# First pair's weight sums on GpSimd, one quarter sum later, and two kinds of request earlier, in an attention and FFN kernel

## Chip, core and metric

One core of a Trainium2 chip runs the whole kernel. The metric is the device time of one execution in microseconds (us); lower is better. Five engines work side by side: TensorE (PE, with its weight loads as PEld), VectorE (DVE), ScalarE (ACT), GpSimd (POOL) and SyncE (SP), which here only issues transfers. Each runs its own instructions strictly in the order in which they were queued, and an instruction that waits for a semaphore holds back everything behind it on that engine.

## What is computed

A linear attention over 8 x 8 heads of 576 tokens, and then a feed-forward layer over all 4608 tokens:

```python
def phi(x):
    proj = np.einsum('bhsd,df->bhsf', x, w_phi)
    proj = proj - np.max(np.abs(proj), axis=-1, keepdims=True)
    return np.concatenate([np.exp(proj), np.exp(-proj)], axis=-1)
q_p, k_p = phi(q), phi(k)
kv = np.einsum('bhsf,bhsd->bhfd', k_p, v)
num = np.einsum('bhsf,bhfd->bhsd', q_p, kv)
den = np.einsum('bhsf,bhf->bhs', q_p, np.sum(k_p, axis=2))[..., None] + 1e-06
x = (num / den).transpose(0, 2, 1, 3).reshape(4608, 512)
h = x @ w_in                                    # 512 -> 2048
g = np.maximum(h, 0.0) + alpha * np.minimum(h, 0.0)
out = g @ w_out                                 # 2048 -> 512
```

## The kernel before

Up to about 340 us the attention runs, 32 pairs of heads one after the other; its output goes to `x_d` in DRAM, and the two weights, decoded on the way, to `u_d` and `v_d`. What matters here is what follows, the feed-forward layer. Its tokens are nine chunks of 512 columns. Every fp32 operand is split into a rounded high part (a cast on ACT, `rnd`, L139) and a low part (the original less the high one, on DVE, `low`, L143), and a product is three matmuls, high by high, low by high, high by low (L546 to L548, L556 to L558, and L833 to L835).

**Chunk 0 is done plainly**, from 340 to 422 us. Hidden blocks of 128 rows alternate between an up step of 12 matmuls (`up2`, L546 to L548), the activation (`act_g`: r on ACT at L258, g on DVE at L262, high part gh on ACT, low part gl on DVE), and a down step of 12 matmuls (`down2`, L556 to L558) on gh and gl.

**Chunks 1 to 8 are done as four pairs** with a Strassen-Winograd scheme: seven products in place of eight. A pair has an up phase of eight units (`unit`). The seven products of a unit run in the order A12, S2, S1, S3, then the first product A11 of the next unit, then S4 and A22; pa, pb and pc are their PSUM tiles, and between the products ACT copies (COPY pb<-pa at L889, u and p at L845) and applies r (L853), while DVE adds (L849) and makes g (L854). A down phase (`down_pair`) follows, seven products over eight operands hv each; an operand is a cast on ACT and a low on DVE, now and then with a subtract on DVE.

**The scheme needs sums of weight quarters** besides the plain ones. `sums` makes one set: load the four quarters with a DMA from `a_d` on POOL's queue (L675); four 128x256 adds and subtracts on DVE (`two` and `four`, L682, L683, L688, L689); two halves, each a cast on ACT and a low on DVE (`half0`, `half1`); and two stores on POOL's queue (L703) to `us_d` and `vs_d`. Up-weight sums are su, down-weight sums sv. There are 16 sets: the first nine, in `work[:9]`, are made during chunk 0 at places that a table of offsets, `SUMT`, gives; the last seven (sv of units 6 and 7, su of units 3 to 7) are made during the first pair's up phase. For those su sets unit 3 to 7 of the first pair reads S1 to S4 straight from the halves that the set leaves in SBUF. `"hv" in late` is true for exactly these seven.

**x for the next pair** is loaded during a down phase: `prepare` gives, for each of j = 0 and 1, a load of the first half (xr, L760), and seven pieces, each an optional subtract (L778), a cast to xo and a low; the first piece also asks for the second half. One entry is taken from that list after each operand that `PIECES` names. From the second pair on, the loads of j = 0 and j = 1 share one buffer, so xr_1 is asked for only when DVE has read the last of xr_0.

**What sets the order:** PE, SP and POOL run as the program is written. ACT and DVE are reordered by the framework's scheduler, which holds, with `behind`, the sums and pieces behind the newest instruction of that engine. So a change in one place can move rows of ACT and DVE nearby.

Of the kernel before, what the change touches and what calls it, by code (L numbers as in the profile page):

```python
# [12 lines left out]
ALU = mybir.AluOpType  # L13
# [13 lines left out]
NU = NF // 2  # L27
# [8 lines left out]
NLAST = 4  # L36
NNEXT = 5
UX = 2
PIECES = [(k, u) for k in range(1, 7) for u in range(NU)][4 : 4 + 48 : 3]
NPRE = 2  # L40
W_BUFS = 2
RW_BUFS = 4
# [62 lines left out]
HEAD = 4  # L105
# [5 lines left out]
UPA = 2  # L111
SUM0, SUMD = 1.5, 3.0
SUMT = dict(load=-5.0, two=0.0, four=0.2, half0=0.6, half1=0.8, store0=1.5, store1=1.6)
SUMS = [(0, 0), (0, 1), (1, 0), (1, 1), (2, 0), (2, 1), (3, 1), (4, 1), (5, 1), (6, 1), (7, 1)]
NSUM = 9
NJIT = 3
# [5 lines left out]
def fused_kernel(ctx: ExitStack, tc: tile.TileContext, kq, v, w_phi, w_in, w_out, alpha, out):  # L122
    nc = tc.nc
    act, dve, pool, pe = nc.scalar, nc.vector, nc.gpsimd, nc.tensor
# [9 lines left out]
    def f(t):  # L134
        return t.bitcast(F32)

    def rnd(eng, dst, src):
        if eng is act:
            return act.copy(dst, src)  # L139
        return eng.tensor_copy(dst, src)  # L140

    def low(eng, dst, src, hi):
        return eng.tensor_tensor(dst, src, f(hi), op=ALU.subtract)  # L143
# [13 lines left out]
    late = {}  # L157
# [92 lines left out]
    def behind(eng):  # L250
        return tc.issue_after(newest[eng].ins) if eng in newest and "pso" in late else ExitStack()
# [343 lines left out]
    todo = []  # L595
# [19 lines left out]
    def load_up(p, u):  # L615
        if p:
            parts = (("wa", 2, A11, 2), ("ws", 2, S1, 3), ("ws", 2, S3, 3), ("wb", 1, A22, 2))
        else:
            parts = (("wa", 2, A11, 2), ("ws", 2, A21, 3))
        for tag, k, n, bufs in parts:  # L620
            if p == 1 and u >= NJIT and tag == "ws":
                continue
            t = late["wu"].tile([P, k, 2, WN], F32R, tag=tag, name=f"{tag}{p}_{u}_{n}", bufs=bufs)
            src = us_d[u, :, UPL[n] : UPL[n] + k] if n >= S3 else u_d[u, :, n : n + k]
            nc.sync.dma_start(f(t), src)
            for j in range(k):
                wu[p, u, {S1: (S1, S2), S3: (S3, S4)}.get(n, (n, n + 1))[j]] = t[:, j]
# [31 lines left out]
    def sums(u, down):  # L659
        k = "v" if down else "u"  # L660
        st = {}

        def new(n):
            name = f"s{k}_{u}_{n}"
            if "hv" in late:
                if n and not down:
                    return late["wu"].tile([P, 4 * WN], F32, tag="ws", name=name, bufs=3)
                return late["hv"].tile([P, 4 * WN], F32, tag="hv", name=name, bufs=NH)
            if n:
                return w1t.tile([P, 4 * WN], F32, tag="wraw", name=name, bufs=RW_BUFS)  # L670
            return late["s"].tile([P, 4 * WN], F32, tag="s", name=name, bufs=3)

        def load():
            a = new(0).rearrange("p (n c) -> p n c", n=4)
            pool.dma_start(a, a_d[int(down), u])  # L675
            st["b"] = [a[:, n] for n in ((0, 2, 1, 3) if down else (A11, A12, A21, A22))]
            st["src"] = (a[:, 0:2], a[:, 2:4]) if down else (a[:, 1:3], a[:, 0:4:3])

        def two():
            a11, a12, a21, a22 = st["b"]  # L680
            with behind("dve"):
                dve.tensor_tensor(a22, a21, a22, op=ALU.add)  # L682
                dve.tensor_tensor(a21, a11, a21, op=ALU.subtract)  # L683

        def four():
            a11, a12, a21, a22 = st["b"]
            with behind("dve"):
                dve.tensor_tensor(a11, a22, a11, op=ALU.subtract)  # L688
                dve.tensor_tensor(a12, a12, a11, op=ALU.subtract)  # L689

        def half(n):
            a = st["src"][n]
            t = st[n] = new(n + 1).bitcast(F32R).rearrange("p (n t c) -> p n t c", t=2, c=WN)
            with behind("act"):
                rnd(act, t[:, :, 0], a)
            with behind("dve"):
                low(dve, t[:, :, 1], a, t[:, :, 0])
            if "hv" in late and not down:
                for j, s in enumerate(((S1, S2), (S3, S4))[n]):
                    wu[1, u, s] = t[:, j]  # L700

        def store(n):
            pool.dma_start((us_d, vs_d)[down][u, :, 2 * n : 2 * n + 2], f(st[n]))  # L703

        parts = dict(load=load, two=two, four=four)
        parts |= {f"half{n}": lambda n=n: half(n) for n in range(2)}
        return parts | {f"store{n}": lambda n=n: store(n) for n in range(2)}
# [6 lines left out]
    def glu2(c, ff, n):  # L714
        r = gq[c, ff][n]()
        if n == 3:
            gq[c, ff] = r
# [34 lines left out]
    def prepare(p):  # L752
        c = 2 * p - 1
        todo = []
        for j in range(2):
            b = {}
            cut = p == 1 and not j

            def half(k, b=b):
                (pool if p == 1 else nc.sync).dma_start(b["raw"][:, k], b["src"][:, k])  # L760

            def load(j=j, b=b, cut=cut, half=half):
                raw = late["x2" if j and p == 1 else "xt"].tile([P, 2, 2 * C2], F32, tag="xr", name=f"xr{p}_{j}", bufs=1)
                src = x_d.rearrange("(k j) p s -> j p k s", j=2)[j][:, :, c * C2 : (c + 2) * C2]
                b["raw"], b["src"] = raw, src
                if not cut:
                    half(0)
                for k in range(2):
                    for t in range(2):
                        b[k, t] = raw[:, k, t * C2 : (t + 1) * C2]  # L770

            def quarter(k, t, j=j, b=b):
                nc.sync.dma_start(b[k, t], x_d[2 * k + j, :, (c + t) * C2 : (c + t + 1) * C2])

            def piece(n, src, x=None, j=j, b=b):
                if x is not None:
                    with behind("dve"):
                        dve.tensor_tensor(b[src], b[x[0]], b[x[1]], op=ALU.subtract)  # L778
                t = late["xo"].tile([P, 2, C2], F32R, tag=f"x{n}_{j}", name=f"xo{p}_{n}_{j}")
                with behind("act"):  # L780
                    rnd(act, t[:, 0], b[src])
                with behind("dve"):
                    low(dve, t[:, 1], b[src], t[:, 0])
                xo[p, n, j] = (t[:, 0], t[:, 1])

            steps = [(A11, (0, 0)), (S1, (0, 0), ((0, 1), (0, 0))), (A12, (1, 0)), (S4, (1, 1))]
            steps += [(S3, (0, 1), ((1, 1), (0, 1))), (S2, (1, 1), ((1, 1), (0, 0))), (A22, (1, 0), ((1, 0), (1, 1)))]
            todo.append(load)
            if cut:
                todo += [lambda k=k, t=t, quarter=quarter: quarter(k, t) for k in range(2) for t in range(2)]  # L790
            more = [] if cut else [half]
            for st_ in steps:
                todo.append(lambda st_=st_, piece=piece, more=more: ([h(1) for h in more[:1]], more.clear(), piece(*st_)))
        return todo

    order = [("u", k) for k in range(HEAD)]
# [5 lines left out]
    for n, (k, ff) in enumerate(order):  # L802
        t = HEADS[n] if n < HEAD else t1 + (n - HEAD) * U2
        if k == "d":
            todo.append((t, lambda ff=ff: down2(ff)))
            if ff + 2 * NPRE < NF:
                todo.append((max(t + 0.0005, (WDT + (0,) * NF)[ff]), lambda ff=ff + 2 * NPRE: load_down(ff)))
            continue
        todo.append((t, lambda ff=ff: up2(0, ff)))
        if n >= HEAD and ff % 2 and ff // 2 + UPA < NU:  # L810
            todo.append((t + 0.0006, lambda u=ff // 2 + UPA: load_up(0, u)))
        for i, dt in enumerate(GH.get(ff, (0, *GQ))):
            todo.append((t + U2 - 0.01 + dt, lambda ff=ff, i=i: glu2(0, ff, i)))
    for u in range(NOWN, HEAD // 2 + UPA):
        todo.append((t1 + 0.0001 + 2.5 * U2 * (u > NOWN), lambda u=u: load_up(0, u)))
    work = [sums(*x) for x in SUMS] + [sums(u, 0) for u in range(NJIT, NU)]
    for n, parts in enumerate(work[:NSUM]):
        for k, dt in SUMT.items():
            todo.append((max(t1 + 0.0002, t1 + (SUM0 + SUMD * n + dt) * U2 + 0.002), parts[k]))
    for n, t in enumerate(XPT + tuple(t1 + (XP0 + XPD * n) * U2 + 0.003 for n in range(11))):  # L820
        todo.append((t, lambda n=n: (prep.extend(prepare(1) if n == 0 else []), pieces(1))))
    todo.append((t1 + 5 * U2, lambda: prep.pop(4)()))
    end = t1 + (len(order) - HEAD) * U2 - 0.002
    todo.append((end, lambda: load_up(1, 0)))
    todo.append((end + 10, turn_on))
    todo.sort(key=lambda tu: tu[0])
    for late_part, engines in ((False, pinned), (True, {et.PE, et.SP, et.Pool})):
# [90 lines left out]
    hv, wv = {}, {}  # L918
# [36 lines left out]
    def down_pair(p):  # L955
# [4 lines left out]
        for k, n in enumerate(ORDER):  # L960
# [8 lines left out]
            for u, m in um:  # L969
# [11 lines left out]
                if m == turn and k + u:  # L981
                    some_operand()
                    if (k, u) in PIECES:
                        pieces(1)
# [117 lines left out]
```

## Time and profile before

| | us |
|---|---|
| median of 3 runs | 1013.92 (1013.58 to 1015.92) |
| the profiled execution | 1014.1 |
| its span | 1012.3 |
| PE busy in the span | 994.4 |
| DVE busy | 787.8 |
| ACT busy | 606.6 |
| POOL busy | 242.0 |

The span runs from the first instruction to the last; 1.8 us lie around it. Busy time counts the time in which an engine executes something; an engine's idle time before an instruction is put down to what that instruction waited for last. The granted clock is TensorE's, as a share of full speed.

### The profile page before, as it was taken

How to read it: one execution, taken by the hardware profiler on the slowest of the kernel's cores; microseconds unless marked ns; L12 is line 12 of the kernel's file. 1: busy time of each engine (PE TensorE's matmuls, PEld its weight loads, DVE VectorE, ACT ScalarE, POOL GpSimd, SP SyncE). 2: the span in 40 equal slices, each digit the busy share in tenths (PEclk: the TensorE clock that was granted, in tenths of full speed). 3: DMA queues.
4: the chain of work that ended last, by engine and by line, in shares of the span. 5: the costliest groups of instructions: out<-in, count | busy, mean ns of one | idle time of the engine just before them, and what ended most of it. 6: DMA issues, size and time to landing. Idle time of an engine off the chain costs nothing.

```text
span 1012.3 us, 18434 instructions
## 1 busy us (share of the span) xinstructions
PE 994.4 (98%) x6881; PEld 804.6 (79%) x6881; DVE 787.8 (78%) x1238; ACT 606.6 (60%) x1163; POOL 242.0 (24%) x218
## 2 busy tenths in 40 slices
PE   9999999999999989999999999999999999999998
PEld 7666666766676878887888888888888888888887
DVE  7999999999997767689997565897465887465874
ACT  4787878787786534455565444566454565444553
POOL 0565656666575322122000000000000000000001
PEclk9999999999999999999999999999999999999999
DMA  5677888898886599988768665768566768565565
GB/s 178 214 282 273 290 282 294 278 331 293 293 288 215 186 352 408 398 307 336 284 223 272 201 217 194 264 223 273 183 229 222 253 207 307 175 210 196 180 220 182
DMA packets 99336, 258.47 MB, mean 255 GB/s; under 512 B 12656, under 2 KB 13296, under 8 KB 99248
## 3 DMA queue, kind: packets, MB, share of 16 engines
q1 hardware_dynamic: 88816, 221.71, 64.1%
q0 software_dynamic: 10000, 35.39, 9.1%
q8 instruction: 54, 0.88, 0.4%
q14 instruction: 34, 0.28, 0.1%
q10 hardware_dynamic: 432, 0.20, 0.1%
HBM read 196.16 MB, written 60.96 MB: 254 GB/s over the span
## 4 chain that ended last, share of the span: by engine, by line
PE 83%; DVE 4%; DMA 3%; ACT 0%; issue 0%; SPq 0%; ACTq 0%; DVEq 0%
PE kv L387 5%; PE n L452 5%; PE qa L835 5%; PE qa L834 5%; PE qa L833 5%; PE pa L833 5%; PE pa L834 5%; PE pa L835 5%; PE pj L347 4%; PE pc L835 3%; PE pc L834 3%; PE pc L833 3%; PE qc L835 2%; PE d L470 2%; PE qc L833 2%; PE qc L834 2%
## 5 line engine op out<-in xcount | busy, mean ns | idle before, releaser
L139 ACT CAST hv<-g 128x512 fp32r<-128x512 f32 x224 | 135.8, 619 | 88.4 <-PE qa L835 43.7
L143 DVE TENSOR_TENSOR hv<-g,hv 128x512 fp32r<-128x512 f32 x224 | 150.8, 687 | 42.0 <-ACT hv L139 41.1
L725 POOL DMA_DIRECT2D out_dram<-pt x35 | 19.0, 543 | 504.6 <-ACT pt L1001 416.7
L835 PE MATMUL qa<-hv,wv 128*128 128x512 f32 (+1 forms) x257 | 97.3, 379 | 0.0
L834 PE MATMUL qa<-hv,wv 128*128 128x512 f32 (+1 forms) x257 | 97.2, 378 | 0.0
L833 PE MATMUL qa<-hv,wv 128*128 128x512 f32 (+1 forms) x257 | 97.2, 378 | 0.0
L351 DVE TENSOR_REDUCE m<-pj 128x8 f32<-128x1024 f32 (+2 forms) x67 | 78.3, 1169 | 5.3 <-PE pj L347 5.3
L352 DVE TENSOR_TENSOR t<-pj,m 128x1024 f32<-128x1024 f32 (+2 forms) x67 | 78.9, 1177 | 4.4
L347 PEld LDWEIGHTS pj<-w_sb,raw 64*128 64x128 f32 x1024 | 63.2, 190 | 17.5 <-issue 13.9
L200 POOL TENSOR_TENSOR aw<-ew,aw 128x512 f32<-128x512 f32 x32 | 41.1, 1285 | 143.3 <-DVE ew L196 143.3
L347 PE MATMUL pj<-w_sb,raw 64*128 64x128 f32 x1024 | 72.7, 282 | 2.3 <-DVE t L352 1.8
L374 POOL TENSOR_TENSOR y<-xk 128x1024 f32<-128x1024 f32 x30 | 70.9, 2364 | 0.0
L452 PE MATMUL n<-qf,sf 128*64 128x288 f32 x512 | 69.2, 412 | 0.0
L366 ACT ACTIVATE xk<-t 128x1024 f32<-128x1024 f32 (+1 forms) x66 | 65.8, 1072 | 4.9 <-DVE t L352 4.9
L443 ACT ACTIVATE qf<-qt 128x512 f32<-128x512 f32 x128 | 66.7, 633 | 0.0
L853 ACT ACTIVATE r<-g 128x512 f32<-128x512 f32 x65 | 37.4, 622 | 47.4 <-DVE g L849 47.4
L387 PE MATMUL kv<-xk,v 128*64 128x256 f32 x512 | 62.3, 385 | 0.0
L463 ACT COPY s<-n 128x288 f32<-128x288 f32 x64 | 25.3, 399 | 58.3 <-PE n L452 58.3
L854 DVE SCALAR_TENSOR_TENSOR g<-r,al,g 128x512 f32<-128x512 f32 x65 | 46.3, 748 | 17.8 <-ACT r L853 17.8
L139 ACT CAST xo<-xr 128x512 fp32r<-128x512 f32 x56 | 34.1, 621 | 40.0 <-DVE xr L778 19.7
L835 PEld LDWEIGHTS qa<-hv,wv 128*128 128x128 f32 x257 | 48.6, 189 | 7.1 <-DVE hv L143 0.2
L833 PEld LDWEIGHTS qa<-hv,wv 128*128 128x128 f32 x257 | 48.6, 189 | 6.9
(195 smaller groups left out, 2586.3 us busy)
## 6 DMA issues: line engine op xcount, KB each, us to landing
wv<-vs_d SPq DMA_DIRECT2D x64, 512.0 KB, 4.4
ws<-us_d SPq DMA_DIRECT2D x54, 512.0 KB, 4.7
wv<-v_d SPq DMA_DIRECT2D x48, 512.0 KB, 4.3
wa<-u_d SPq DMA_DIRECT2D x37, 512.0 KB, 6.2
raw<-kq_dram SPq DMA_DIRECT2D x31, 576.0 KB, 5.0
v<-v_dram SPq DMA_DIRECT2D x32, 320.0 KB, 4.2
rr<-rec_d SPq DMA_DIRECT2D x64, 144.0 KB, 3.2
x_d<-rr SPq DMA_DIRECT2D x32, 288.0 KB, 2.5
```

Of the source, the lines that this page charges most:

```text
L139: return act.copy(dst, src)
L143: return eng.tensor_tensor(dst, src, f(hi), op=ALU.subtract)
L347: pe.matmul(dst[h, j], lhsT=c["raw"][hs, ts], rhs=w_sb[hs], start=True, stop=True)
L351: dve.tensor_reduce(m, src, axis=AX.X, op=ALU.max, apply_absolute_value=True)
L352: dve.tensor_tensor(t[:, hs, js], src, m.unsqueeze(3).broadcast_to([P, nh, nj, FD]), op=ALU.subtract)
L374: pool.tensor_tensor(y, x[:, :, : 2 * FD], x[:, :, 2 * FD :], op=ALU.add)
L387: pe.matmul(c["kv"][h * D : (h + 1) * D, 0:2], lhsT=c["v"][:, tp, h, :], rhs=c["x", ch][:, :, h, j, :], start=tp == 0, stop=tp == NV - 1,)
L443: act.activation(c["qf"][:, h, a, : 4 * P], ps.rearrange("p j f -> p (j f)"), AF.Exp, scale=sg)
L452: pe.matmul(ps[h * D : (h + 1) * D, :], lhsT=c["st"][:, a, h * D : (h + 1) * D], rhs=c["qf"][:, h, a, u * HS : (u + 1) * HS], start=a == 0 ...
L833: pe.matmul(ps, lhsT=wh, rhs=xh, start=first, stop=False, skip_group_check=True)
L834: pe.matmul(ps, lhsT=wl, rhs=xh, start=False, stop=False, skip_group_check=True)
L835: pe.matmul(ps, lhsT=wh, rhs=xl, start=False, stop=end, skip_group_check=True)
```

## The change

Four edits:

1. The four adds of a set go to POOL for the seven sets of the first pair (`adder`). The other nine stay on DVE.
2. For the set n = 1 of the table (sv of unit 0), the second half and its store come at 2.2 and 2.6 slots instead of 0.8 and 1.6 (`SUML`).
3. The first pair's first weights, `load_up(1, 0)`, are asked for at an entry of chunk 0's table, behind the up step of block 13, instead of at the table's end.
4. In the down phases the entries of the x list are taken at `PIECES[1::3]` instead of `[4:52:3]`, three operands sooner; for pairs 2 to 4 an empty entry in front of j = 1's pieces keeps the last ones where they were.

```diff
-PIECES = [(k, u) for k in range(1, 7) for u in range(NU)][4 : 4 + 48 : 3]
+PIECES = [(k, u) for k in range(1, 7) for u in range(NU)][1::3]
...
+SUML = dict(half1=2.2, store1=2.6)
...
+        def adder():
+            return (pool, ExitStack()) if "hv" in late else (dve, behind("dve"))
+
         def two():
             a11, a12, a21, a22 = st["b"]
-            with behind("dve"):
-                dve.tensor_tensor(a22, a21, a22, op=ALU.add)
-                dve.tensor_tensor(a21, a11, a21, op=ALU.subtract)
+            eng, order = adder()
+            with order:
+                eng.tensor_tensor(a22, a21, a22, op=ALU.add)
+                eng.tensor_tensor(a21, a11, a21, op=ALU.subtract)
...
             todo.append(load)
+            if p > 1 and j:
+                todo.append(lambda: None)
...
-        if n >= HEAD and ff % 2 and ff // 2 + UPA < NU:
-            todo.append((t + 0.0006, lambda u=ff // 2 + UPA: load_up(0, u)))
+        if n >= HEAD and ff % 2 and ff // 2 + UPA <= NU:
+            u = ff // 2 + UPA
+            todo.append((t + 0.0006, lambda x=(0, u) if u < NU else (1, 0): load_up(*x)))
...
-        for k, dt in SUMT.items():
+        for k, dt in (SUMT | SUML if n == 1 else SUMT).items():
             todo.append((max(t1 + 0.0002, t1 + (SUM0 + SUMD * n + dt) * U2 + 0.002), parts[k]))
...
-    todo.append((end, lambda: load_up(1, 0)))
```

`four` is changed in the same way as `two`. The lines of the changed kernel are numbered a few higher.

The queues around unit 3 of the first pair, POOL first. Here sv_0_5584 is the set of down weights of unit 7, su_0_5586 the set of up weights of unit 3; _1 and _2 are their two halves. Before:

```order
L675 DMA su_0_5668<-a_d 128x1024 [waits DMASW4_49,DMASW2_49]
L703 DMA vs_d<-sv_1_5674 128x1024 [waits DMASW3_49,DVE_49]
L703 DMA vs_d<-sv_2_5719 128x1024 [waits DVE_49]
L675 DMA su_0_5755<-a_d 128x1024 [waits DMASW5_49,DMASW1_49]
L703 DMA us_d<-su_1_5761 128x1024 [waits DMASW6_49]
```

and after:

```order
L695 TENSOR_TENSOR sv_0_5584<-sv_0_5584 128x256 [waits Pool_49]
L709 DMA vs_d<-sv_1_5674 128x1024 [waits DMASW3_49,DVE_49]
L709 DMA vs_d<-sv_2_5719 128x1024 [waits DVE_49]
L676 DMA su_0_5755<-a_d 128x1024 [waits Pool_49]
L687 TENSOR_TENSOR su_0_5586<-su_0_5586 128x256 [waits DMASW6_49]
L688 TENSOR_TENSOR su_0_5586<-su_0_5586 128x256 [waits Pool_49]
L694 TENSOR_TENSOR su_0_5586<-su_0_5586 128x256 [waits Pool_49]
L695 TENSOR_TENSOR su_0_5586<-su_0_5586 128x256 [waits Pool_49]
L709 DMA us_d<-su_1_5761 128x1024 [waits DVE_49]
```

The four adds of the set su_0_5586 now stand on POOL behind two stores that wait for DVE and behind a load.

ACT in the same place (pb_3 is unit 3's copy of pa; r_1_2 and r_1_3 are activations of units 2 and 3). Before:

```order
L889 COPY pb_2_5731<-pa_2_5724 128x512 [waits PE_49]
L139 CAST su_1_5761<-su_0_5586 128x2x256 [waits DMAHW3_49,DMAHW0_49,DMAHW4_49,DMASW6_49,DMAHW7_49,DVE_49,PE_49]
L853 ACTIVATE r_1_1_5740<-g_1_5691 128x512 [waits DVE_49,Activation_49]
...
L139 CAST su_2_5803<-su_0_5586 128x2x256 [waits DMAHW7_49,DMAHW2_49,DMAHW0_49]
L139 CAST sv_1_5674<-sv_0_5584 128x2x256 [waits DMASW5_49,DMASW0_49]
L139 CAST sv_2_5719<-sv_0_5584 128x2x256 [waits DVE_49]
L889 COPY pb_3_5815<-pa_3_5808 128x512 [waits PE_49]
```

and after:

```order
L140 CAST sv_1_5674<-sv_0_5584 128x2x256 [waits DMASW5_49,DMASW0_49,Pool_49]
L897 COPY pb_3_5815<-pa_3_5808 128x512 [waits DVE_49,PE_49]
L140 CAST sv_2_5719<-sv_0_5584 128x2x256 [waits DMASW1_49,Pool_49]
...
L861 ACTIVATE r_1_3_5860<-pb_3_5815 128x512 [waits DVE_49,PE_49]
L140 CAST su_1_5761<-su_0_5586 128x2x256 [waits DMAHW3_49,DMAHW4_49,DMAHW0_49,DMAHW7_49,DMASW6_49,Pool_49]
L140 CAST su_2_5803<-su_0_5586 128x2x256 [waits DMAHW2_49,DMAHW7_49,DMAHW0_49,Pool_49]
L853 COPY u_1_3_5869<-pa_3_5808 128x512 [waits PE_49]
```

The cast of unit 3's S1 and S2 moved from behind COPY pb_2 to behind COPY pb_3 and two more sets of rows, and the cast sv_2_5719 moved behind COPY pb_3. Further down, in the same way, the casts su_1_5845 and su_2_5887 come to stand ahead of COPY pb_4 of the next unit, and su_2_5887 waits there for the landing of the store of su_1_5761 (its buffer).

ACT during chunk 0, at hidden block 4 (r_0_4 and gh_0_4 belong to its activation, sv_2 is the second half of set n = 1). Before:

```order
L139 CAST sv_1_4989<-sv_0_4865 128x2x256 [waits DMASW1_49,DMAHW5_49,DVE_49,Activation_49]
L139 CAST sv_2_4994<-sv_0_4865 128x2x256 [waits DMAHW5_49,DVE_49,Activation_49]
L258 ACTIVATE r_0_4_4967<-h_0_4_4950 128x512 [waits PE_49]
L139 CAST gh_0_4_5000<-g_0_4_4992 128x512 [waits DVE_49]
L139 CAST xo_7_0_5024<-xr_0_2889 128x512
```

and after:

```order
L140 CAST sv_1_4989<-sv_0_4865 128x2x256 [waits DMASW1_49,DMAHW5_49,DVE_49,Activation_49]
L259 ACTIVATE r_0_4_4967<-h_0_4_4950 128x512 [waits PE_49]
L140 CAST gh_0_4_4997<-g_0_4_4992 128x512 [waits DVE_49]
L140 CAST xo_7_0_5020<-xr_0_2889 128x512
L140 CAST sv_2_5023<-sv_0_4865 128x2x256 [waits DMAHW5_49,Activation_49]
```

The second half's cast stands behind the activation of block 4 instead of ahead of it; its low on DVE moved in the same way behind g, gl and xo_7.

In the down phase, on SP, before (xr_1 is the load of x with j = 1):

```order
L927 DMA wv_4_2_6638<-vs_d 128x2x512 [waits DMAHW0_49,PE_49]
L927 DMA wv_4_3_6668<-vs_d 128x2x512 [waits DMAHW1_49,PE_49]
L760 DMA xr_1_6688<-x_d 128x1024 [waits DVE_49]
L927 DMA wv_5_0_6690<-vs_d 128x2x512 [waits DMAHW2_49,PE_49]
L927 DMA wv_5_1_6710<-vs_d 128x2x512 [waits DMAHW3_49,PE_49]
```

and after:

```order
L935 DMA wv_4_2_6642<-vs_d 128x2x512 [waits DMAHW0_49,PE_49]
L766 DMA xr_1_6653<-x_d 128x1024 [waits DVE_49]
L935 DMA wv_4_3_6670<-vs_d 128x2x512 [waits DMAHW1_49,PE_49]
L935 DMA wv_5_0_6690<-vs_d 128x2x512 [waits DMAHW2_49,PE_49]
L935 DMA wv_5_1_6710<-vs_d 128x2x512 [waits DMAHW3_49,PE_49]
```

xr_1's first half is asked for one weight load sooner. On ACT its first cast, xo_2_1, moved from behind the casts of hv_4_6 and hv_4_7 to ahead of them. SP's rows for `load_up(1, 0)` stand where they stood.

## Rows read from the trace of the kernel before

**Rows 1.** The page: busy time, share of the span and instructions of each engine.

```profile
PE 994.4 (98%) x6881; PEld 804.6 (79%) x6881; DVE 787.8 (78%) x1238; ACT 606.6 (60%) x1163; POOL 242.0 (24%) x218
```

**Rows 2.** Waits of PE, 330 to 1000 us: total, times, longest.

```profile
PE po L556 <- ACT gh L139: 3.2, 1, 3.2
PE qc L835 <- DVE hv L143: 2.9, 3, 1.3
PE pa L833 <- DVE g L854: 1.7, 1, 1.7
PE pa L833 <- DMA wa<-u_d: 1.4, 1, 1.4
```

**Rows 3.** Timeline of chunk 0, block 4: start, duration, instruction, idle before and releaser.

```profile
357.61 0.62 ACT L139 CAST sv<-sv 128x512 fp32r<-128x512 f32 x1 [3.80 <-DMA v_d<-raww]
...
358.26 0.69 DVE L143 TENSOR_TENSOR sv<-sv,sv 128x512 fp32r<-128x512 f32 x1 [3.72 <-ACT sv L139]
...
360.31 0.48 PE L556 MATMUL po<-gh,wd 128*128 128x512 f32 x1 [3.16 <-ACT gh L139]
```

**Rows 4.** Stretches: length, busy time of each engine (instructions), granted clock, DMA share, GB/s.

```profile
core 0: us, PE busy (x) PEld busy (x) DVE busy (x) ACT busy (x) POOL busy (x), PEclk, DMA share, GB/s
350.00:375.00 25.00, 21.81 (x93) 18.17 (x92) 15.48 (x26) 8.73 (x15) 8.81 (x13) 0.93 0.97 345
...
400.00:426.00 26.00, 26.00 (x121) 22.47 (x120) 20.42 (x37) 14.57 (x27) 5.85 (x11) 1.00 1.02 411
...
361.40:364.80 3.40, 3.40 (x10) 2.68 (x9) 2.72 (x6) 0.83 (x2) 0.00 (x0) 0.50 1.04 389
...
451.00:493.00 42.00, 40.27 (x187) 34.79 (x186) 37.92 (x67) 25.29 (x47) 7.64 (x15) 1.00 0.91 325
```

**Rows 5.** Timeline: the first pair's first weights reach PE.

```profile
414.35 0.19 PEld L833 LDWEIGHTS pa<-xo,wa 128*128 128x128 f32 x1 [0.39 <-DMA wa<-u_d]
```

**Rows 6.** Timeline of the first pair, units 3, 4 and 6: copies and products.

```profile
447.73 0.57 ACT L889 COPY pb<-pa 128x512 f32<-128x512 f32 x1
...
451.41 0.38 PE L833 MATMUL pa<-xo,su 128*128 128x512 f32 x1
...
456.79 0.57 ACT L889 COPY pb<-pa 128x512 f32<-128x512 f32 x1 [2.00 <-PE pa L835]
...
475.41 0.48 PE L833 MATMUL pa<-xo,wa 128*128 128x512 f32 x1 [1.73 <-DVE g L854]
```

**Rows 7.** POOL's groups by line, and one DVE group of 428 to 493 us: count, busy, mean ns.

```profile
L374 POOL TENSOR_TENSOR y<-xk 128x1024 f32<-128x1024 f32 x30 | 70.9, 2364 | 0.0
L200 POOL TENSOR_TENSOR aw<-ew,aw 128x512 f32<-128x512 f32 x32 | 41.1, 1285 | 143.3 <-DVE ew L196 143.3
L703 POOL DMA_DIRECT2D us_d<-su x16 | 8.5, 535 | 30.3 <-DVE su L143 30.1 <-issue 0.2
...
L854 DVE SCALAR_TENSOR_TENSOR g<-r,al,g 128x512 f32<-128x512 f32 x14 | 10.2, 747 | 0.8 <-ACT r L853 0.8
...
L683 DVE TENSOR_TENSOR su<-su 128x256 f32<-128x256 f32 x5 | 2.1, 422 | 0.1
```

**Rows 8.** Timeline: an add on POOL and an add on DVE at the same time.

```profile
351.27 1.56 POOL L501 TENSOR_TENSOR rr<-s,rr 128x576 f32<-128x576 f32 x1 [7.98 <-DMA rr<-rec_d]
...
351.60 1.52 DVE L688 TENSOR_TENSOR sv<-sv 128x256 f32<-128x256 f32 x1
```

**Rows 9.** Stores of su, 440 to 480 us: time from issue to landing.

```profile
DMA to landing us min/median/max: 2.9/6.7/11.4
```

**Rows 10.** Timeline of the first pair's down phase: load, cast, low, PE.

```profile
538.28 0.46 SPq L760 DMA_DIRECT2D xr<-x_d  x1
...
546.55 0.62 ACT L139 CAST xo<-xr 128x512 fp32r<-128x512 f32 x1 [4.17 <-DMA xr<-x_d]
...
547.20 0.69 DVE L143 TENSOR_TENSOR xo<-xr,xo 128x512 fp32r<-128x512 f32 x1 [4.10 <-ACT xo L139]
...
555.34 0.48 PE L835 MATMUL qc<-hv,wv 128*128 128x512 f32 x1 [1.34 <-DVE hv L143]
```

More of the change, by code (lines that the diff above doesn't have):

```diff
@@ L677, in load @@
             st["src"] = (a[:, 0:2], a[:, 2:4]) if down else (a[:, 1:3], a[:, 0:4:3])
+        def adder():
+            return (pool, ExitStack()) if "hv" in late else (dve, behind("dve"))
         def two():
             a11, a12, a21, a22 = st["b"]
-            with behind("dve"):
-                dve.tensor_tensor(a22, a21, a22, op=ALU.add)
-                dve.tensor_tensor(a21, a11, a21, op=ALU.subtract)
+            eng, order = adder()
+            with order:
+                eng.tensor_tensor(a22, a21, a22, op=ALU.add)
+                eng.tensor_tensor(a21, a11, a21, op=ALU.subtract)
         def four():
             a11, a12, a21, a22 = st["b"]
-            with behind("dve"):
-                dve.tensor_tensor(a11, a22, a11, op=ALU.subtract)
-                dve.tensor_tensor(a12, a12, a11, op=ALU.subtract)
+            eng, order = adder()
+            with order:
+                eng.tensor_tensor(a11, a22, a11, op=ALU.subtract)
+                eng.tensor_tensor(a12, a12, a11, op=ALU.subtract)
         def half(n):
```

## Prediction, made before the changed kernel had run

> **What bounds the kernel now.** First the page: PE is busy 994.4 of 1012.3 us [rows 1]. What an edit gives or costs is therefore read from the gaps of PE, not from the busy time of the engine that it relieves. Second, who PE waits for after 330 us [rows 2]: 3.2 us once for ACT's cast gh, 2.9 us in three pieces for DVE's low of hv, 1.7 us once for DVE's g, 1.4 us once for a load of weights, 9.2 us in all. Third, the timeline around each gap, to see which instruction stood in front of the one that PE waited for [rows 3, 5, 6, 10]. Fourth, stretches with the clock and the DMA share [rows 4]: only once after 330 us is the clock low, 0.50 in 361.40 to 364.80, right behind the 3.16 us gap; 3.4 us at 1.2 instead of 2.4 GHz lose about 1.7 us, and behind the gap of 1.73 us no such stretch lies.
>
> **Edit 2, the quarter sum in chunk 0.** It removes a block. ACT stood 3.80 us in front of the cast of sv because that cast waits for the landing of a store; r of block 4 stood behind it on ACT and g behind the low of sv on DVE, which sat idle 3.72 us, then gh, and PE waited 3.16 us for that [rows 3]. With the cast behind gh, r and g need not wait for the landing, and the half clock has no gap to follow. PE would then lead the old times by some 3.2 + 1.7 = 4.9 us. The lead is spent on the way. The DMA share is 0.97 from 350 to 375 us and 1.02 from 400 to 426, with 345 and 411 GB/s [rows 4], and the first weights of the first pair came just when PE wanted them: PE's weight load waited 0.39 us for wa and began at 414.35 [rows 5]. A DMA system without a pause can't deliver sooner, and edit 3 doesn't help, as SP's rows stand in the same order. The only reserve is the 0.03 x 25 = 0.75 us by which the share of 350 to 375 stays below one. I take -0.5 us. Ends: -4.9 if other transfers can give way to the weights, and +2 if the lead is lost in one gap over 3 us, with another stretch of low clock.
>
> **Edit 1, POOL adds in the first pair.** It removes 28 adds of 0.42 us, 11.8 us, from DVE [rows 7], and with them the 1.73 us at 475.41, where PE waited for DVE's g [rows 2, 6]: DVE is busy 37.92 of 42 us from 451 to 493 [rows 4]. So -1.7 us.
>
> What it adds is 28 adds on POOL. The trace has none of 128x256; 128x1024 takes 2.36 and 128x512 1.29 us [rows 7], on a straight line 0.75 us for 128x256, 3.0 us for the four of a set. POOL has room; its order is the trouble. I follow unit 3's S2, which reads the half su_1 of the set su_0_5586. Before, DVE did it early and PE began S2 at 451.41 without a wait [rows 6]. After, its four adds stand on POOL behind the stores of sv_1_5674 and sv_2_5719, and the second of these waits for a cast that ACT does behind COPY pb_3. The copy starts at 447.73 and takes 0.57 [rows 6], to 448.3; the cast 0.62 and low 0.69 [rows 3], to 449.6; the store and the next load, 0.54 each, as the stores of us_d [rows 7], to 450.7; four adds, 3.0, to 453.7; the cast of su_1, 0.62, to 454.3. PE wants it at 451.41: a wait of 2.9, and 0.4 more before the second matmul, which needs the low part: 3.3 us. While the adds run, DVE makes two g of 0.75 from SBUF [rows 7]; that one engine holds the other up is seen at 351.60, where an add of DVE took 1.52 instead of 0.42 while POOL ran 1.56 [rows 8]. If the two g hold up POOL in the same way, it is 3.3 + 1.5 = 4.8. I take 4.0. A gap of this size is nearer to the 3.16 us gap than to the 1.73 one, so I add a stretch of low clock, 1.7 us, with 0 as the other end.
>
> The next term is unit 4. The cast of su_2_5887 now stands ahead of COPY pb_4 and waits for the landing of the store of su_1_5761. Stores here take 2.9 to 11.4 us, 6.7 in the middle [rows 9]. The store goes out at about 455.5, so it lands between 458.4 and 466.9, at 462.2 in the middle; the copy of unit 4 came at 456.8, one unit of seven products or 9.1 us after that of unit 3 [rows 6], and with the delays above (4.0 + 1.7) is wanted at 462.5. PE waits nothing at the middle and 4.4 at the upper end; I take 1.5. Units 5 to 7 have the same shape with POOL now three adds behind; 0 to 3.5, I take 0.5. Sum of edit 1: -1.7 + 4.0 + 1.7 + 1.5 + 0.5 = +6.0 us, with ends at +1.6 (no clock, 3.3 and nothing else) and +13.
>
> The Trainium skill, "SBUF — State Buffer", section "SBUF: two separate sides", says that a DVE instruction with two inputs in SBUF and a GpSimd instruction that reads SBUF exclude each other for the whole instruction. The row at 351.60 fits this. By the rule the 28 adds would shut DVE's lows and subtracts out whenever they meet; that outcome is the second rival.
>
> **Edit 4, x in the down phases.** PE waits 1.34 us at 555.34 and 2.9 in the three down phases that load x [rows 2, 10]. The cause stands earlier: the load of xr_1 is issued at 538.28, the cast of xo waits 4.17 us for it to 546.55, and DVE 4.10 us behind the cast [rows 10]; casts and lows of hv queue behind that and PE reaches the deficit nine us later. After, the load is issued one weight load sooner, which is two operands of 1.3 us each (a unit's 9.1 us over its seven products) or 2.6 us, at about 535.7, and it lands at 544.0 if it takes the same 8.2 us, sooner if the queue is shorter by then. The cast of xo_2_1 also stands two operands sooner, which gives back 2 x 1.3 us of the gain, and the block then holds two more casts of hv. But j = 0's pieces are done three operands sooner, which empties the bunch behind. At least the bunch starts 2.6 us sooner; the deficit was 1.34. I take -2.5 of the 2.9. Ends: -2.9, and +1 if the cast blocks longer than it did.
>
> **Edit 3** changes no queue order: 0. The 1.4 us wait for a load at unit 1 [rows 2] hangs on a transfer behind PE's own S1 of unit 0 and stays.
>
> **Sum.** -0.5 + 6.0 - 2.5 + 0 = +3.0 us on the profiled 1014.1: 1017.1, say 1017.0. The profiled run is 0.2 over the median of 1013.92. A difference of 0.3%, about 3.0 us, is what a measurement can tell from none; the forecast lies on that bound.
>
> **The rivals.**
> - *POOL's chain is cheap* (no change). The gap at unit 3 is 3.3, no low clock follows, the store lands in time: edit 1 costs -1.7 + 3.3 = +1.6, and 1014.1 + 1.6 - 0.5 - 2.5 = 1012.7. For it: PE's wait is broken in two pieces, 2.9 and 0.4, and stores can land in 2.9 us. Against it: the gap is as long as the one that the half clock followed.
> - *DVE and POOL exclude each other* (slower). 28 adds of 0.75 are 21 us of POOL. If DVE is kept out of them for most of that, it loses up to 21 - 11.8 = 9 us more than it was given, and it has only 42 - 37.9 = 4.1 us idle from 451 to 493 [rows 4]. PE then waits for g and for su in several units: some 5 us on top of the forecast, 1022. It decides from the point where DVE loses more than its 4 idle us. Against it: most of DVE's g and adds there take one input from PSUM.
> - *The lead is kept* (faster). Transfers that nobody waits for give way in chunk 0 and PE keeps 4 to 5 us; with the cheap chain that is 1012.7 - 4.4 = 1008.3, with the forecast's chain 1012.6. For it: the sums' loads and stores share the engines with the weights and have slack. Against it: 0.39 us of wait at 414.35 with the share at 1.02.
> - *The change does not do what it says* in edit 3, which is in the sum already, or in edit 4: the cast that moved ahead blocks hv_4_6 as long as before, and the 2.5 stays. Then 1019.5.
>
> **How the numbers follow.** The forecast's case 0.42, over the bound in about 0.27 of it; cheap chain 0.20; exclusion 0.17; lead kept with a cheap chain 0.17; edit 4 void 0.04. Slower 0.27 + 0.17 + 0.04 = 0.48; faster 0.17; within 0.3% the other 0.35. The range leaves out about a tenth at each side: below, half of the case at 1008.3 and its lower end; above, the upper end of edit 1 (+13) and more than one stretch of low clock. 1009 to 1023.
>
> **What the profile after would show.** Edit 1: a PE wait of 3 to 5 us at unit 3's S2, put down to ACT's cast of su or DVE's low, with POOL's adds just before it, the granted clock at 0.5 behind it, and no wait of PE for g in unit 6. POOL adds of 0.75 us, longer where DVE works from SBUF. Unit 4: a COPY pb held up behind a cast that waits for a store. Edit 2: no wait at block 4 and full clock, but waits of PE for wa, wd or gh between 375 and 415, and pa's first weight load again at about 414. Edit 4: PE's waits for hv gone, or moved to hv_4_6. The prediction is wrong if PE reaches the first pair 2 us or more sooner, if unit 3's S2 doesn't wait, or if POOL's adds are as short as DVE's.

## The result, and the profile after

The changed kernel takes 1022.82 us, the median of five runs (1019.82 to 1023.08), beside 1015.92 for the kernel before in the same session: a ratio of 1.0069, 95% interval 1.0049 to 1.0088, some 7 us slower. The profiled execution took 1021.94 us with a span of 1020.2, which is 7.9 us over that of before. The page's line of busy times, in answer to [rows 1]:

```profile
PE 997.7 (98%) x6881; PEld 805.9 (79%) x6881; DVE 787.5 (77%) x1210; ACT 606.8 (59%) x1163; POOL 267.7 (26%) x246
```

DVE has 28 instructions fewer and is busy as long as before. Of the 11.6 us that the adds took, 6.4 us came back in longer instructions (the g of L862 take 807 ns in the mean, where they took 748); for the rest, neighbouring instructions overlap less, which the busy time counts once. The waits of PE from 330 to 1010 us (who for whom: total, times, longest), in answer to [rows 2]:

```profile
PE pa L841 <- DMA wa<-u_d: 3.3, 2, 1.9
PE pa L841 <- ACT su L140: 3.1, 1, 3.1
PE pa L841 <- ACT u L853: 2.8, 3, 1.5
PE po L557 <- ACT gh L140: 2.4, 1, 2.4
PE qc L843 <- DVE hv L144: 1.6, 3, 0.8
PE pa L841 <- DVE g L862: 0.4, 1, 0.4
PE pa L841 <- DMA ws<-us_d: 0.2, 1, 0.2
```

These are 13.8 us in place of 9.2. The rest of the loss is low clock, which shows in a table of stretches (length, busy time of each engine, granted clock, DMA share, GB/s):

```profile
core 0: us, PE busy (x) PEld busy (x) DVE busy (x) ACT busy (x) POOL busy (x), PEclk, DMA share, GB/s
379.80:383.50 3.70, 3.66 (x9) 2.91 (x10) 3.15 (x5) 2.65 (x5) 0.77 (x2) 0.54 1.03 419
455.60:462.00 6.40, 6.35 (x15) 4.73 (x16) 1.45 (x3) 1.70 (x4) 4.63 (x8) 0.52 1.02 393
```

Two stretches at 1.2 GHz, one in chunk 0 and one at unit 3, where before had one [rows 4]. PE's instructions stand in the same order in both kernels, so the same matmul's start in both traces tells where the time went.

**Chunk 0.** The timeline of the changed kernel (start, duration, instruction, idle before and releaser), in answer to [rows 3, 5]:

```profile
356.51 0.38 PE L557 MATMUL po<-gh,wd 128*128 128x512 f32 x1
...
376.19 0.43 DVE L687 TENSOR_TENSOR sv<-sv 128x256 f32<-128x256 f32 x1 [5.62 <-DMA sv<-a_d]
...
379.17 0.62 ACT L140 CAST gh<-g 128x512 fp32r<-128x512 f32 x1 [6.17 <-DVE g L263]
...
379.84 0.78 PE L557 MATMUL po<-gh,wd 128*128 128x512 f32 x1 [2.35 <-ACT gh L140]
...
415.24 0.48 PE L841 MATMUL pa<-xo,wa 128*128 128x512 f32 x1 [1.95 <-DMA wa<-u_d]
```

Block 4 goes on at 356.51 instead of 360.31, without a wait and at full clock. Twenty us later DVE stands 5.62 us in front of an add whose quarters are still being loaded, ACT 6.17 us behind DVE, and PE 2.35 us behind ACT, with low clock after it. At the first pair's first weights PE waits 1.95 us and begins at 415.24, 0.9 us later than before. The lead is gone. The 0.9 us themselves are no loss that can be put down to an edit: in the run of edit 4 alone, whose chunk 0 is that of before, the first pair begins at 415.27.

**Unit 3.** POOL, DVE, ACT and PE of the changed kernel, in answer to [rows 6]:

```profile
450.78 0.53 POOL L709 DMA_DIRECT2D vs_d<-sv  x1 [1.20 <-DVE sv L144]
451.30 0.54 POOL L676 DMA_DIRECT2D su<-a_d  x1
451.86 0.74 POOL L687 TENSOR_TENSOR su<-su 128x256 f32<-128x256 f32 x1
452.67 1.06 POOL L688 TENSOR_TENSOR su<-su 128x256 f32<-128x256 f32 x1
453.81 1.05 POOL L694 TENSOR_TENSOR su<-su 128x256 f32<-128x256 f32 x1
454.95 0.73 POOL L695 TENSOR_TENSOR su<-su 128x256 f32<-128x256 f32 x1
...
451.84 2.44 DVE L862 SCALAR_TENSOR_TENSOR g<-r,al,g 128x512 f32<-128x512 f32 x2 [0.76 <-ACT r L861]
...
454.38 0.60 ACT L861 ACTIVATE r<-pb 128x512 f32<-128x512 f32 x1 [0.25 <-DVE g L862]
454.90 0.62 ACT L140 CAST su<-su 128x512 fp32r<-128x512 f32 x1
...
455.57 0.79 PE L841 MATMUL pa<-xo,su 128*128 128x512 f32 x1 [3.07 <-ACT su L140]
```

The store that waits for DVE, the load, the adds, the cast, PE: the chain as it was followed, but for two things. The cast needs only three of the four adds; the third ends at 454.86, and the fourth runs beside the cast. And ACT's own queue ends in the same place: the r that stands ahead of the cast starts at 454.38, behind DVE's g. An add alone takes 0.73 to 0.74 us; beside the two g of DVE it takes 1.05, and those two take 2.44 us together where each took 0.75 [rows 7].

**Units 4 and 5.** DVE, ACT and PE of the changed kernel:

```profile
466.23 2.57 DVE L144 TENSOR_TENSOR hv<-g,hv 128x512 fp32r<-128x512 f32 x2
468.72 1.21 DVE L949 TENSOR_TENSOR g<-g 128x512 f32<-128x512 f32 x1
469.85 1.21 DVE L862 SCALAR_TENSOR_TENSOR g<-r,al,g 128x512 f32<-128x512 f32 x1
...
471.16 0.60 ACT L861 ACTIVATE r<-pa 128x512 f32<-128x512 f32 x1 [3.67 <-DVE g L862]
...
472.29 0.48 PE L841 MATMUL pa<-xo,su 128*128 128x512 f32 x1 [1.52 <-ACT u L853]
```

Four instructions of DVE in a row, with both inputs in SBUF, take about 1.2 to 1.3 us each while POOL adds; ACT stands 3.67 us behind them, the copy u that PE waits for stands behind ACT's r. The first three of the four, two lows and a subtract for the down phase, stood behind the unit's four g in the kernel before; now they stand ahead of them. Before:

```profile
459.53 0.75 DVE L854 SCALAR_TENSOR_TENSOR g<-r,al,g 128x512 f32<-128x512 f32 x1
...
464.06 0.69 DVE L143 TENSOR_TENSOR hv<-g,hv 128x512 fp32r<-128x512 f32 x1
```

So this wait has two causes, the longer instructions and DVE's new order, and no run parts them. By the same matmuls PE is 0.9 us behind the kernel before at 415, 4.2 when S2 of unit 3 begins, 7.5 at the end of the low clock, 11.2 at 483, and 9.8 at 493 (483.50 before, 493.26 after).

**The down phases** give 1.9 us of that back: PE waits 0.23, 0.57 and 0.81 us for hv where it was 1.34, 1.33 and 0.27 [rows 2, 10].

### The profile page after: what moved, and what is told of

The parts are those of the page before. It is cut to its first block, busy times and chain, and to the rows that moved or that the text cites. A ratio compares the mean times of both kernels' runs of the same rounds, so it can differ in the third digit from the quotient of the medians.

```text
span 1020.2 us, 18441 instructions
## 1 busy us (share of the span) xinstructions
PE 997.7 (98%) x6881; PEld 805.9 (79%) x6881; DVE 787.5 (77%) x1210; ACT 606.8 (59%) x1163; POOL 267.7 (26%) x246
## 4 chain that ended last, share of the span: by engine, by line
PE 79%; DMA 7%; DVE 4%; issue 1%; ACT 1%; SPq 0%; POOL 0%; DVEq 0%; ACTq 0%; POOLq 0%
PE kv L388 5%; PE n L453 5%; PE pa L841 5%; PE pa L842 5%; PE pa L843 5%; PE qa L843 5%; PE qa L842 5%; PE qa L841 5%; PE pj L348 4%; PE pc L843 3%; PE pc L842 3%; PE pc L841 3%; DMA wa<-u_d 3%; PE d L471 2%; PE qc L843 2%; PE qc L842 2%
## 5 line engine op out<-in xcount | busy, mean ns | idle before, releaser
L862 DVE SCALAR_TENSOR_TENSOR g<-r,al,g 128x512 f32<-128x512 f32 x65 | 49.9, 807 | 19.3 <-ACT r L861 19.3
```

## The experiments

Ratios are to the kernel before, run on the same chip in the same session, with 95% intervals.

**Edit 1 alone** (`adds_only`): the function `adder` and nothing else.

> The kernel before with edit 1 alone: the adds of the first pair's seven sets on POOL. Theory (POOL's order delays unit 3's S2, and low clock and DVE's blocking follow): the whole loss of the changed kernel is here, +8 to +9 us between 450 and 500 us, ratio to before 1.007 to 1.010. Rival (the loss needs the four edits together, since chunk 0 brings PE and the transfers to the first pair at other times): under +4 us, ratio 1.000 to 1.004.

Measured 1.0076 (1.0064 to 1.0088). Its waits of PE from 330 us on:

```profile
PE po L556 <- ACT gh L139: 3.3, 1, 3.3
PE pa L838 <- ACT su L139: 3.1, 1, 3.1
PE pa L838 <- ACT u L850: 2.9, 3, 1.5
...
```

The 3.3 us are those of before in chunk 0; the other two lines are those of the changed kernel. Edit 1 is the whole loss. One of the three waits for hv in the down phases is gone as well (1.23, 0 and 0.27 us), without edit 4.

**Edit 2 alone** (`quarter_only`): the table `SUML` and its use.

> The kernel before with edit 2 alone: the second half of one quarter sum later in chunk 0. Theory (transfers bound chunk 0, so a lead of PE is spent until the first pair's first weights land at about 415 us): the 3.16 us gap at 360 is gone, another wait stands between 375 and 416, and the time is within -0.5 to +2 us, ratio 0.9995 to 1.002. Rival (a gap of PE is worth its length and the low clock behind it): -5 us, ratio 0.995.

Measured 0.9997 (0.9985 to 1.0009). PE's two waits between 375 and 416 in its trace:

```profile
379.60 0.48 PE L557 MATMUL po<-gh,wd 128*128 128x512 f32 x1 [2.14 <-ACT gh L140]
...
414.66 0.48 PE L834 MATMUL pa<-xo,wa 128*128 128x512 f32 x1 [2.68 <-DMA wa<-u_d]
```

A gap of 3.16 us with the low clock behind it is taken out, and nothing is gained: 2.14 and 2.68 us of waiting stand where the lead is spent, and the first pair begins at 414.66 instead of 414.35.

**Edit 4 alone** (`x_only`).

> The kernel before with edit 4 alone: the x pieces three operands sooner. Theory: the three waits for hv, 2.9 us in sum, shrink to some 1 to 1.6 us and nothing else moves: -1.3 to -2 us, ratio 0.998 to 0.9987. Rival (the smaller waits of the changed kernel came from its other edits): no change, ratio 1.000.

Measured 1.0000 (0.9988 to 1.0011): the theory failed. Its trace around the first down phase:

```profile
541.53 0.62 ACT L139 CAST xo<-xr 128x512 fp32r<-128x512 f32 x1 [0.77 <-DMA xr<-x_d]
...
551.17 1.66 ACT L139 CAST xo<-xr 128x512 fp32r<-128x512 f32 x3 [2.58 <-DMA xr<-x_d]
...
551.17 0.69 DVE L778 TENSOR_TENSOR xr<-xr 128x512 f32<-128x512 f32 x1 [3.15 <-DMA xr<-x_d]
...
556.12 0.48 PE L837 MATMUL qc<-hv,wv 128*128 128x512 f32 x1 [1.33 <-DVE hv L143]
```

The wait for the first half of xr fell from 4.17 to 0.77 us, as it was meant to. Then the third piece needs the second half, which is asked for with the first piece, no sooner than before, and ACT and DVE wait 2.58 and 3.15 us for that. PE's wait is the 1.33 us that it was.

**All but edit 1** (`no_adds`): `adder` returns DVE.

```diff
-            return (pool, ExitStack()) if "hv" in late else (dve, behind("dve"))
+            return dve, behind("dve")
```

> The changed kernel with edit 1 undone: DVE adds in the first pair, edits 2 to 4 kept. Theory (effects add up): about the sum of edits 2 and 4, -2 to +1 us against before, ratio 0.998 to 1.001, and no wait at unit 3's S2. Rival (edit 2's lead is kept when POOL does no adds): -5 to -7 us, ratio 0.993 to 0.995.

Measured 0.9992 (0.9983 to 1.0001). The parts add up: nothing of the lead is kept without POOL's adds either.

**The same adds, in another place on POOL** (`adds_ahead`): those of the next set stand ahead of the stores of this one.

```diff
-                    for n in ("two", "four", "half0"):
-                        work[u][n]()
+                    for k in (0, 1) if u == 0 else (u + 1,):
+                        if k < len(work):
+                            work[k]["two"]()
+                            work[k]["four"]()
+                    work[u]["half0"]()
```

> The changed kernel with POOL's rows in another order: the four adds of a set stand ahead of the stores of the set before, and so wait for nothing but their load. Theory (the order makes the 3.07 us wait at unit 3 and the low clock behind it): both are gone, 455 us onwards gains 6 us, and what is left is DVE held up by POOL's reads, 1 to 3 us in units 4 to 7: ratio to before 1.000 to 1.003. Rival (POOL and DVE excluding each other is the cost, whatever the order): waits of the same size in units 3 to 6, ratio 1.006 to 1.008.

Measured 1.0011 (0.9997 to 1.0024). The adds of unit 3's set, PE at unit 3's S2, and the stretches behind it:

```profile
438.80 0.73 POOL L687 TENSOR_TENSOR su<-su 128x256 f32<-128x256 f32 x1
...
451.75 0.38 PE L841 MATMUL pa<-xo,su 128*128 128x512 f32 x1
...
450.00:462.00 12.00, 12.00 (x57) 10.50 (x56) 7.77 (x11) 6.80 (x13) 9.08 (x13) 1.00 1.00 351
462.00:485.00 23.00, 20.80 (x93) 16.96 (x92) 22.28 (x31) 13.29 (x25) 13.76 (x19) 1.00 0.80 275
```

The same 28 adds, 13 us earlier for this set: S2 begins at 451.75 without a wait, PE is busy without a break to 462 at full clock. The waits that are left, 0.39, 0.67, 0.94 and 0.21 us from 467 to 480, 2.2 us in sum, fall where DVE is busy 22.28 of 23 us. So the order made most of the loss. ACT's cast of the set came forward with the adds (443.75 instead of 454.90), as the scheduler placed it; POOL's order and ACT's are not told apart by this run.

**POOL's adds beside DVE, by themselves** (`pool_reads`), and **memsets of the same length** (`pool_memsets`): in the kernel before,

```diff
+                    for _ in range(4):
+                        pool.tensor_tensor(scr[:, :256], scr[:, 256:], scr[:, 256:], op=ALU.add)
                     for n in ("two", "four", "half0"):
                         work[u][n]()
```

and in the second `for _ in range(6): pool.memset(scr, 0.0)`.

> The kernel before, with the sums on DVE as they were, and 28 adds of 128x256 on POOL over a scratch tile of zeros that nobody waits for, four in front of each set's stores. It prices POOL's reads beside DVE alone. Theory (POOL and DVE take turns, each add and each DVE instruction with two SBUF inputs up to 0.7 us longer): DVE, 90% busy here, loses 5 to 9 us, PE waits for g or su more than the 1.73 us of before, ratio 1.003 to 1.008. Rival (holding up happens, but beside idle time): the 1.73 us wait as before, ratio 1.000 to 1.001.

> The same as the run with idle POOL adds, but with 42 memsets of 128x512, about as long in sum, in place of the 28 adds: POOL writes and reads nothing. Theory (only POOL's reads hold up DVE): DVE's adds and lows keep 0.42 and 0.69 us, ratio 1.000 to 1.001. Rival (any POOL work, or its place ahead of the stores, costs): as much as the adds.

Measured 1.0065 (1.0048 to 1.0082) with the adds and 1.0002 (0.9988 to 1.0015) with the memsets. Groups of 428 to 493 us (POOL's to 500): count, busy, mean ns. First of the adds, then of the memsets:

```profile
L1035 POOL TENSOR_TENSOR scr<-scr 128x256 f32<-128x256 f32 x28 | 21.4, 766 | 1.8
L854 DVE SCALAR_TENSOR_TENSOR g<-r,al,g 128x512 f32<-128x512 f32 x12 | 10.9, 939 | 1.5 <-ACT r L853 1.5
L854 DVE SCALAR_TENSOR_TENSOR g<-r,al,pa 128x512 f32<-128x512 f32 x6 | 4.4, 736 | 0.0
L683 DVE TENSOR_TENSOR su<-su 128x256 f32<-128x256 f32 x5 | 2.6, 528 | 0.0
```

```profile
L1035 POOL MEMSET scr<- 128x512 f32 x42 | 22.2, 529 | 2.0
L854 DVE SCALAR_TENSOR_TENSOR g<-r,al,g 128x512 f32<-128x512 f32 x14 | 10.2, 751 | 1.5 <-ACT r L853 1.5
L683 DVE TENSOR_TENSOR su<-su 128x256 f32<-128x256 f32 x5 | 2.1, 424 | 0.0
```

With adds on POOL, g takes 939 ns instead of 747 [rows 7] and DVE's add 528 instead of 422; with memsets of 22.2 us in sum, 751 and 424. The g that take one input from PSUM (pa) are not held up: 736 ns, 744 in the kernel before. So POOL's adds, which read SBUF, hold up the DVE instructions with both inputs there; POOL's time and its place in the queue alone don't. The Trainium skill, "SBUF — State Buffer", section "SBUF: two separate sides", says that a DVE instruction with two SBUF inputs and a GpSimd instruction that reads SBUF exclude each other, and that the one that starts second is held for the whole of the other. The two runs agree on which instructions meet, but the changed kernel's trace shows less than a full hold: at unit 3 two g and two adds, 3.0 us in sum where each runs alone, took 2.44 us together. In the memset run PE's 1.4 us wait at unit 1 is gone too: there a store and the memset that clears the scratch tile stand ahead of the first pair's three set loads, these go out 3 us later, and wa came in time. The run with adds shares this, so the two differ in the kind of POOL's work alone.

**Both halves of xr_1 together** (`x_both`), and **the second half one weight load behind the first** (`x_mid`), both without edit 1.

> The changed kernel without edit 1, and with both halves of xr_1 asked for together instead of the second with the first piece. Theory (with edit 4 the second half, which is asked for no sooner, takes over as what ACT and DVE wait for, 2.58 and 3.15 us in its trace alone): no wait over 1 us for xr and PE's three waits for hv, 2.9 us in sum, gone; against before -2 to -3.5 us, ratio 0.9965 to 0.998. Rival (the queue of casts and lows behind is simply too long): waits as before, ratio 0.999 to 1.000.

> The changed kernel without edit 1, with the second half of xr_1 asked for at the empty entry, one weight load behind the first half, where asking for both at once had delayed weight loads by 1.0 to 1.3 us. Theory (the wait for hv goes with an earlier second half, the wait for wv with a weight load between the halves): PE's waits for hv and wv in the three down phases under 1.5 us in sum, -1.5 to -2.5 us against before, ratio 0.9975 to 0.9985. Rival (what casts gain, weights lose): ratio 0.9995 to 1.001.

Measured 1.0016 (1.0001 to 1.0030) and 1.0031 (1.0019 to 1.0044): neither gives anything. With both halves together the waits for hv are gone, and two for weights, 2.3 us in sum, behind the x loads in the queue, take their place. With a weight load between them the waits for hv are many and small: seven for DVE's low, 1.7 us in sum, and two for ACT's cast, 1.0 us. The sum is 2.3 to 2.7 us, 2.9 before. That the medians are higher by 2 to 3 us is not explained by these waits; it stays open. The traces are of executions 1.4 and 1.7 us under their medians and may not show it.

**Four more transfers in chunk 0** (`dma_more`): `pool.dma_start(scr_d[n], a_d[0, n])` four times.

> The kernel before with four more transfers of 512 KB from DRAM to DRAM on POOL's queue, into a tile that nobody reads, spread over chunk 0 from its first sums on. Theory (transfers bound chunk 0, share 0.95 to 1.03): each takes 512 KB / 410 GB/s = 1.3 us from the others, the first pair's first weights land some 5 us later than 414.3, and the time is 4 to 6 us longer, ratio 1.004 to 1.006. Rival (there is slack, and the lead was lost to ACT and DVE waiting for one load alone): under 2 us, ratio 1.000 to 1.002.

Measured 1.0033 (1.0022 to 1.0044), less than the 1.004 to 1.006 that was expected and more than the rival's 1.002: the first pair begins at 416.59, 2.2 us later where some 5 were expected, behind two waits of PE for wa (0.91 and 1.53 us). Transfers do move the end of chunk 0, but not each one of them in full.

**The ninth set later** (`one_set_later`), and **all sets a place later** (`sums_later`), both with edit 2 (in the second for the first set):

```diff
-NSUM = 9
+NSUM = 8
...
+    work.append(work.pop(8))
```

and, in the second, besides `SUM0 = 4.5` for 1.5.

> Edit 2 alone, and with it the ninth set of sums (sv of unit 5) made at the end of the first pair's up phase instead of in chunk 0: one load and two stores, 1.5 MB or some 3.8 us of transfers, leave chunk 0, and four adds and two lows, 3.1 us of DVE, come to the first pair. Theory (PE's lead in chunk 0 is kept as far as transfers leave): the first pair begins 3 to 4 us sooner than with edit 2 alone, about 411 instead of 414.66; what the first pair's DVE then makes of it is open, ratio 0.996 to 1.001. Rival (something else than transfers holds PE to 414): it begins within 1 us of 414.66.

> The run with the ninth set moved, and besides all sets of chunk 0 one place later (SUM0 4.5 instead of 1.5, the late half now that of the first set), so that a whole set, 1.5 MB, is asked for behind the first pair's first weights instead of ahead of them. The set that was moved alone was the last of chunk 0, whose transfers stood behind those weights anyway, and they still landed at 414.25. Theory (transfers queued ahead of the first pair's weights set its begin): the first pair begins 2.5 to 4 us sooner than 414.25, and the time is 0.994 to 0.998 of before. Rival (PE is held to 414 by something else, or the transfers fall between the first units instead): begin within 1 us of 414.25, or a wait as long behind it, ratio 0.998 to 1.000.

Measured 0.9985 (0.9971 to 0.9998) and 0.9985 (0.9972 to 0.9997): some 1.5 us faster than the kernel before, if at all, as the intervals end just below 1. Neither did it as expected. In the first the first pair begins at 414.25, the rival's number; the gain is behind it, where the waits of before at 437 and 475 are gone. In the second:

```profile
374.70 0.48 PE L557 MATMUL po<-gh,wd 128*128 128x512 f32 x1 [1.90 <-ACT gh L140]
...
371.98 0.43 DVE L683 TENSOR_TENSOR su<-su 128x256 f32<-128x256 f32 x1 [4.61 <-DMA su<-a_d]
...
375.00:379.00 4.00, 4.00 (x11) 2.89 (x10) 2.76 (x5) 1.94 (x4) 0.70 (x2) 0.57 1.02 419
...
413.85 0.38 PE L835 MATMUL pa<-xo,wa 128*128 128x512 f32 x1
```

PE no longer waits for wa: it begins at 413.85 without a gap. But a set's add waits 4.61 us for its load and holds g, gh and PE as in the changed kernel, with low clock behind it, and that spends the lead instead, so the begin is again the rival's. The trace is of the fastest of twelve executions, 1009.69 us, where the median is 1013.52.

## Why the prediction was right, and where its steps were not

The direction and the place were right: slower, and by edit 1 at unit 3. The size was not: +3.0 was forecast and some 7 measured, and the time lies 0.2 us under the upper end of the range. The figure in the prediction that came nearest is the second rival's, 1022, and that is in part luck: its mechanism is seen at units 4 and 5, but the run with the adds ahead has the same 28 adds at 1.1 us over the kernel before, and the rest of the loss came by the forecast's own chain and a longer stretch of low clock. In PE's lag, from 0.5 us ahead at 350 us to 7.9 behind at the end, the parts are +1.4 in chunk 0, +6.6 at S2 of unit 3 with its low clock, +3.7 at units 4 and 5, -1.8 at 475, +0.3 up to 493 and -1.9 in the down phases; the sum had -0.5, +5.7, +2.0 for units 4 to 7, -1.7 and -2.5. Term by term:

- **Edit 1, S2 of unit 3.** The chain was right to a few tenths: 3.07 us of wait and a second piece of 0.4 before the next matmul, where 2.9 and 0.4 were the least, and 4.0 was taken. That is partly luck: the cast needs three adds and not four, and the three took the 3.0 us that four were given, since two of them met DVE's g. The r that ACT does ahead of the cast was not followed at all, and would alone have held the cast to 454.9. The run with the adds ahead shows that the order is the cause of the wait.
- **Its low clock** was sized at 1.7 us and took some 3.0: 15 matmuls in 6.4 us at a granted clock of 0.52, where half that time was needed before, less the 0.4 of the second piece. This is what the sum lacked at this place.
- **Units 4 to 7** were the wrong mechanism. The cast behind the landing of a store cost nothing: the store in question landed after 5.0 us (456.65 to 461.66) and not the 6.7 that was taken, and COPY pb waited for PE. The waits at units 4 and 5 come from DVE and POOL taking turns, which the prediction kept as its second rival, at 5 us on top, and at unit 4 also from DVE's new order, which it left out. By the same matmuls PE loses 3.7 us more from the end of the low clock to 483, nearly twice the 2.0 us that the sum held for these units. The reason against the rival, that most g and adds take one input from PSUM, is true of those and beside the point at unit 4, where four instructions in a row take none.
- **The gain of 1.7 us at 475** did come: the same matmul, at 484.84 in the changed kernel, begins without a wait, and PE's lag falls by 1.8 us there.
- **Edit 2** was right: -0.5 forecast, -0.3 +- 1.2 us measured alone. The reason was half of it. Transfers set the pace, but the lead went first to one late load of a set, through DVE and ACT, and only then to the wait for wa; and in the run with all sums later, where PE no longer waits for wa, the first of these alone spent it. In the changed kernel's own trace chunk 0 ended at +1.4, near the upper end. The stretch of low clock there is not shown to be the reason: in the run without edit 1 the same stretch is there and the first pair begins at 414.50, with edit 2 alone and full clock at 414.66.
- **Edit 4** failed: -2.5 forecast, 0.0 +- 1.2 us measured. The step that failed is the one from "At least the bunch starts 2.6 us sooner" to the end of the deficit: its first cast did start sooner (541.53 instead of 546.55 in the run of edit 4 alone), but of the two loads only the first was followed. The second half was left in its place and became the next thing waited for. The 1.9 us that the changed kernel won in its down phases are no proof of edit 4: with edit 1 alone the three waits are 1.5 us in sum, with edit 4 alone 3.1.
- **Edit 3** was not run alone. Edits 2 to 4 together measured 0.9992, and the order of SP's rows is the same, so nothing is seen of it, as forecast.

Measured alone, edit 1 cost 7.7 us (1.0076) where 6.0 was forecast and edit 4 gave 0 where 2.5 was forecast; these two are the difference between 3 and 7.

## What to carry to other kernels

When work goes to an engine that is mostly idle, look at its queue before its load: an add behind a store that waits for another engine came 13 us later than the same add ahead of it, and that, with the rows of ACT and DVE that the scheduler moved along, was 6 of the 7 us. Sums over SBUF moved from DVE to GpSimd relieve DVE little while it has much to do with two SBUF inputs: it ended as busy as before. And a gap that is removed in a stretch where transfers are busy all the time, or a load of which only the first half is moved, gives the time to the next wait in line.

## What the runs showed of the chip that was not expected

The length of a gap alone doesn't tell whether TensorE's clock falls to 1.2 GHz behind it. It fell after gaps of 1.90 us (all sums later), 2.17 us (without edit 1) and 2.35 us (the changed kernel in chunk 0), and with two gaps of 0.80 and 1.63 us close together in the run with POOL's reads; it did not fall after one of 2.14 us at the same place in the run of edit 2 alone, nor after one of 3.35 us in the run with POOL's reads. Stretches behind three of these gaps, of 2.14, 2.17 and 3.35 us (length, busy time of PE, PEld, DVE, ACT and POOL, granted clock, DMA share, GB/s):

```profile
379.00:384.00 5.00, 4.33 (x18) 3.18 (x19) 3.80 (x7) 3.21 (x6) 1.50 (x3) 1.00 1.03 420
380.30:384.00 3.70, 3.70 (x10) 2.70 (x9) 2.83 (x6) 2.36 (x5) 1.16 (x3) 0.54 1.03 422
480.30:484.00 3.70, 3.67 (x17) 3.25 (x18) 3.70 (x8) 1.69 (x3) 0.96 (x2) 1.00 0.35 142
```

Executions of one kernel differ in this too: with edit 2 alone the mean granted clock was 1.000 in four of twelve and 0.997 to 0.999 in the others, and one stretch like that of before takes 0.002 off the mean. So the prediction's choice by the nearest gap came out right by luck, and no run here tells what decides. Where DVE and POOL meet, both are slower, in turns: POOL's 128x256 add goes from 0.73 to 1.05 us and DVE's g from 0.75 to 1.2 (unit 3). A g with one input in PSUM keeps its time.
